# Attention and MLP in one kernel: MLP groups of six chunks, up products that change PSUM banks half way, probability products in batches of two to four key blocks

## The chip, the core and the metric

The kernel runs on one core of one Trainium2 chip, in one launch. The metric is the device time of that launch in microseconds (us), given as the median of several runs. A profiled execution of the same program gives the trace that is read below; its engines are PE (TensorE: matrix products, with its weight loads listed apart as PEld), DVE (VectorE), ACT (ScalarE), POOL (GpSimd) and SP (SyncE, whose queue issues nearly all DMAs).

## The reference

The input x has 2048 tokens of 576 numbers. Two branches are mixed by a gate per token:

```
g = sigmoid((x * gate_w).sum(-1))
a = attention(x @ wqkv, 32 heads of 18) @ wo
b = gelu_tanh(layernorm(x) @ w1 + b1) @ w2 + b2      (w1: 576 x 4608, w2: 4608 x 576)
out = g * a + (1 - g) * b
```

Attention is a full softmax over 2048 keys for each head. All is float32; the kernel makes its large products out of rounded high parts and rests (hi·hi, hi·lo, lo·hi), so each logical product is three on PE.

## The kernel before

**Stages.** A head (some 216 us) computes q, k, v, the layer norm and the gate. Then comes one long loop of 512 steps: 32 units (a pair of heads and one half of the queries) times 16 key blocks of 128. A tail projects the attention output with wo and adds the MLP branch. The loop is written out in Python, so that the order of every instruction on every engine's queue is fixed when the program is built; each engine takes its instructions in that order.

**A step.** `s2` (L275) makes scores for one key block and 512 queries, two heads side by side on the two halves of PE's rows (a *pair* of products), and ACT takes their exponentials (L278) into a tile of a ring of four, `p_of(n) = RING[n % 4]`. It does so twice per step. After each `s2` stands one *round* `s1_round` (L230) of a later unit: again two products side by side, whose row maxima DVE takes (`tensor_reduce`, L232). These four products a round share five PSUM banks in turn (`score_bank`). `pv` (L293) multiplies the probabilities of several finished steps by v. It uses PE as four column strips of 32, where everything else in the loop uses two row halves of 64. It comes once for every `span[0]` steps: a *batch*. Before, the span is 2 unless an up pair asks for 3.

**The MLP as filler.** The MLP is a generator, `mlp()`, from which `fill` and `atom` draw pieces between the score products. A piece runs up to the next mark (`cut[0] = 1` at a slot in `ends`). `GAPS = 7` pieces fit in a batch of two steps: two in its first step, four in the second, one before the product with v. The work comes in two kinds of unit:

- An *up pair* (`h_pair`, L494): two chunks of 128 hidden channels for 512 tokens. Row half h makes chunk h alone, over nine input blocks of 64 and three products each: 27 slots of two products side by side, each into its own bank. For this both row halves hold the whole normed input, high and low parts, in two tiles `Y[0]`, `Y[1]`; part of the low half stands in a tile `low` for the first token block.
- A *down pair* (`out_pair`, L582): 128 tokens and the 4 chunks of one group, 24 slots of two products. Here row half h holds half of each chunk, so both halves add to both output banks. They may not write one bank at the same time, so they start on different banks and change over after 12 slots. The change is guarded: ACT's queue holds a `sem_inc` that waits for the two last products of the first half (L589), and PE waits for that semaphore before the first product of the second (`nc.tensor.wait_ge(swap, ...)`). With `TURNS = (3, 6, 12, 18, 21)` and the piece at gap 3 skipped (`skip.add(3)`), one round L230 and one pair L275 stand between the end of the first half and the wait.

The MLP goes by token blocks of 512 (four), in each over nine groups of `G = 4` chunks: two up pairs and four down pairs per group. That is 72 up pairs and 144 down pairs. GELU between them runs on ACT and POOL in several steps, issued by `defer` and `queue_end`, which model time by counted slots. Down sums are added to an SBUF accumulator by DVE after each down pair (L599). Weights are split in the first token block (raw loads, ACT, POOL, and a store to DRAM scratch), and reloaded as w (L139) in the other three: up pairs from a pool of 3 tiles, down chunks from a pool of 4. `prep_w2(i)` asks for a group's down chunks once the group before has finished its down pairs.

**Pace.** `TOTAL` is the MLP's time by the author's slot figures (231 ns an up slot, 131 ns a down slot); the MLP is to end at step `FIN` = 500. From step 489 (`PSTEP`) on the tail's loads and first steps are drawn in.

Of the kernel before, what the change touches and what calls it, by code (L numbers as in the profile page):

```python
# [16 lines left out]
P = 128  # L17
# [10 lines left out]
G = 4  # L28
NFC = F // P
NG = NFC // G  # L30
# [12 lines left out]
GAPS = 7  # L43
ROOM = 1152
TURNS = (3, 6, 12, 18, 21)
TAIL = (6, 12, 16, 20)
BUSY = 20
TOTAL = NB * NG * (G // 2 * 27 * 231 + 8 * 3 * G * 131)
# [4 lines left out]
ORDER = (0, 1, 3, 2)  # L53
# [16 lines left out]
def gated_mix_kernel(ctx: ExitStack, tc: tile.TileContext, x, wqkv, wo, w1, b1, w2, b2, gate_w, out):  # L70
# [41 lines left out]
    low = att.tile([P, 5, TB], F32R, name="low")  # L112
# [154 lines left out]
    def s2(u, kc, qb):  # L267
# [9 lines left out]
        for h in range(2):  # L277
            nc.scalar.activation(p_of(n)[:, qb, h], ps[h], AF.Exp, scale=SCALE)  # L278
# [63 lines left out]
    def mlp():  # L342
        W1, W2, HT = {}, {}, {}
        RAW = {}
        seq = [(tb, g) for tb in range(NB) for g in range(NG)]
        n = len(seq)
        npair = n * (G // 2)
        Y, ACC = {}, {}

        def chunk(q):  # L350

            i, m = divmod(q, G // 2)
            return i, m, seq[i][1] * G + 2 * m


        R1, R2 = [], []
        for raws in (x_tile(), x_tile()):
            R1.append(raws[:, :9 * P].rearrange("p (c n) -> p c n", c=9))
            R2.append([raws[:, 9 * P + k * D:9 * P + (k + 1) * D] for k in range(2)])
# [9 lines left out]
        def load_w1(q):  # L369

            if (1, q) in LOADED or q >= NQ0:
                return
            LOADED[1, q] = slot[0] + LAND
            fc = chunk(q)[2]
            for h in range(2):
                src = w1[:, (fc + h) * P:(fc + h + 1) * P]
                nc.sync.dma_start(raw1(q)[64 * h:64 * h + 64], src.rearrange("(c p) n -> p c n", p=64))
# [15 lines left out]
        def split(table, key, pool, shape, raw, src, scr, then):  # L393

            def first():
                LOAD[raw[0]](raw[1])
                t = pool.tile(shape, F32R, name="w" + str(len(shape)))
                nc.scalar.activation(t[:, 0], src, AF.Copy)  # L398
                bg.insert(0, (any_time, lambda: second(t), queue, 0))

            def second(t):
                pool_op(src.free_size(), nc.gpsimd.tensor_tensor, t[:, 1], src, t[:, 0].bitcast(F32), op=ALU.subtract)
# [30 lines left out]
        def prep_w2(i):  # L433
            for m in range(G // 2):
                q = i * (G // 2) + m
# [25 lines left out]
        def cuts(n, pieces):  # L461

            return {(k * n + pieces - 1) // pieces for k in range(1, pieces)}

        def h_pair(q, last, inner=False):

            i, m, fc = chunk(q)
            tb = seq[i][0]
            while q == 0 and q not in W1:
                cut[0] = 3  # L470
                yield 0
            wt = ready(W1, q)
            del W1[q]
            ps = [psum(ps_w) for _ in range(2)]
            if q == 0:
                slots = [(w_, 0, c) for c in range(9) for w_ in (0, 1)] + [(0, 1, c) for c in range(9)]
            else:
# [869 lines left out]
```

## Time and profile before

| | |
|---|---|
| median of 3 runs | 2212.33 us (2211.47 to 2215.21) |
| profiled execution, its own time | 2212.78 us |
| its span in the trace | 2211.0 us, 1.8 us less |
| PE busy | 2197.4 us, 99% |
| DVE, ACT, POOL busy | 75%, 64%, 45% |
| mean granted TensorE clock | 1.000 |
| DMA moved | 329.74 MB, mean 149 GB/s |

An engine's busy time is the union of its instructions. PE's instructions overlap each other (one begins while the one before still drains), so what a product costs is read from the distance between starts rather than from its own length.

### The profile page before, as it was taken

The numbers are of one execution on the slowest core, as the hardware profiler recorded it, in microseconds if no ns is written. First come the engines' busy times: TensorE is split into PE (matmuls) and PEld (weight loads), VectorE is DVE, ScalarE is ACT, GpSimd is POOL, SyncE is SP. The second block draws the span as 40 slices with busy tenths as digits, with TensorE's granted clock in tenths as the row PEclk, the third lists the DMA queues.
The fourth block names the chain that finished last, engine by engine and source line by source line (L and its number), as shares of the span: only waits on it lengthen the run. The fifth ranks groups of instructions, "written<-read, shape, count | busy, mean of one in ns | idle before, by whom it ended". The sixth has DMA issues, their size and how long they took to land.

```text
span 2211.0 us, 51479 instructions
## 1 busy us (share of the span) xinstructions
PE 2197.4 (99%) x20496; PEld 1578.5 (71%) x20496; DVE 1647.9 (75%) x2888; ACT 1425.9 (64%) x2623; POOL 1003.7 (45%) x1000
## 2 busy tenths in 40 slices
PE   8999999999999999999999999999999999999999
PEld 7877666676667776677766777767776777776668
DVE  6675777777778778777777777777776777777734
ACT  4333777777776666666666666666665666666672
POOL 4331766666664444444444444444444444444800
PEclk9999999999999999999999999999999999999999
DMA  8867655444464623333354424233464333242265
GB/s 263 276 217 224 199 175 156 154 160 151 152 198 139 197 101 123 121 124 105 115 173 150 138 81 136 101 125 101 125 176 146 109 113 120 98 153 101 77 224 169
DMA packets 171640, 329.74 MB, mean 149 GB/s; under 512 B 65314, under 2 KB 91614, under 8 KB 160672
## 3 DMA queue, kind: packets, MB, share of 16 engines
q1 hardware_dynamic: 168850, 322.67, 45.2%
q8 instruction: 161, 2.64, 0.5%
q10 hardware_dynamic: 2454, 3.75, 0.5%
q14 instruction: 79, 0.65, 0.1%
q0 software_dynamic: 96, 0.03, 0.0%
HBM read 234.00 MB, written 96.69 MB: 150 GB/s over the span
## 4 chain that ended last, share of the span: by engine, by line
PE 95%; DVE 2%; DMA 1%; issue 0%; POOL 0%; ACT 0%; SPq 0%; DVEq 0%; ACTq 0%; POOLq 0%
PE ps L293 21%; PE ps L582 21%; PE ps L494 20%; PE ps L275 13%; PE ps L230 11%; PE ps L894 3%; PE ps L1229 3%; PE ps L915 2%; DVE m L232 1%; PE ps L770 0%; DMA p<-in_A_wqkv_dram 0%; DMA big<-y_scr 0%; PE ps L897 0%; PE ps L896 0%; DVE st L857 0%
## 5 line engine op out<-in xcount | busy, mean ns | idle before, releaser
L232 DVE TENSOR_REDUCE m<-ps 128x1 f32<-128x512 f32 x2048 | 1311.3, 684 | 390.3 <-PE ps L230 380.3
L278 ACT ACTIVATE p<-ps 128x512 f32<-128x512 f32 x1048 | 568.3, 597 | 301.7 <-PE ps L275 299.3
L278 ACT ACTIVATE ring<-ps 128x512 f32<-128x512 f32 x1000 | 543.2, 596 | 294.9 <-PE ps L275 291.8
L494 PE MATMUL ps<-big,w 64*128 64x512 f32 x3708 | 569.4, 393 | 0.2 <-issue 0.2
L183 POOL TENSOR_SCALAR zz<-zz 128x512 f32<-128x512 f32 x288 | 178.1, 618 | 743.3 <-ACT zz L547 686.1
L582 PE MATMUL ps<-w,hh 64*128 64x288 f32 x4352 | 477.4, 294 | 1.5 <-DVE x L599 1.5
L275 PE MATMUL ps<-qa,ka 56*128 56x512 f32 x2048 | 448.6, 420 | 1.1 <-ACT p L278 0.3
L582 PEld LDWEIGHTS ps<-w,hh 64*128 64x128 f32 x4352 | 417.2, 186 | 32.5 <-DVE x L599 6.2
L230 PE MATMUL ps<-ka,qa 54*128 54x512 f32 x2048 | 425.6, 397 | 0.1
L494 PEld LDWEIGHTS ps<-big,w 64*128 64x128 f32 x3708 | 369.8, 187 | 66.1 <-issue 0.5
L183 POOL TENSOR_TENSOR zz<-zz,z 128x512 f32<-128x512 f32 x288 | 371.4, 1290 | 24.0
L275 PEld LDWEIGHTS ps<-qa,ka 56*128 56x128 f32 x2048 | 204.4, 184 | 226.3 <-DVE m L232 174.7
L582 PE MATMUL ps<-w,hl 64*128 64x288 f32 x2176 | 339.3, 292 | 0.8 <-POOL hl L183 0.8
L293 PE MATMUL ps<-p,vt 128*32 128x512 f32 x1968 | 239.1, 598 | 0.0
L230 PEld LDWEIGHTS ps<-ka,qa 54*128 54x128 f32 x2048 | 213.4, 184 | 22.6 <-DVE m L232 2.6
L293 PE MATMUL ps<-ring,vt 128*32 128x512 f32 x1872 | 227.6, 598 | 0.0
L582 PEld LDWEIGHTS ps<-w,hl 64*128 64x128 f32 x2176 | 222.2, 184 | 1.2 <-POOL hl L183 1.1
L183 POOL TENSOR_TENSOR hl<-zz,hh 128x512 fp32r<-128x512 f32 x136 | 176.6, 1299 | 11.4
L183 POOL TENSOR_TENSOR w<-x,w 128x576 fp32r<-128x576 f32 (+1 forms) x54 | 98.8, 1842 | 164.1 <-ACT w L398 158.4
L293 PEld LDWEIGHTS ps<-p,vt 128*32 128x32 f32 x1968 | 52.5, 109 | 111.8 <-issue 102.7
L293 PEld LDWEIGHTS ps<-ring,vt 128*32 128x32 f32 x1872 | 49.8, 109 | 106.4 <-issue 106.4
L599 DVE SCALAR_TENSOR_TENSOR x<-ps,x 128x288 f32<-128x288 f32 x256 | 103.6, 446 | 8.8 <-PE ps L582 8.4
(121 smaller groups left out, 1538.2 us busy)
## 6 DMA issues: line engine op xcount, KB each, us to landing
w<-w_scr SPq DMA_DIRECT2D x54, 1152.0 KB
w<-w_scr SPq DMA_DIRECT2D x108, 576.0 KB
x<-in_B_w_dram SPq DMA_DIRECT2D x72, 288.0 KB
w_scr<-w SPq DMA_DIRECT2D x18, 1152.0 KB
w_scr<-w SPq DMA_DIRECT2D x36, 576.0 KB
qa<-qk_scr SPq DMA_DIRECT2D x192, 72.0 KB
ka<-qk_scr SPq DMA_DIRECT2D x84, 144.0 KB
qk_scr<-hh SPq DMA_DIRECT2D x36, 256.0 KB
```

The lines of the kernel that those rows point to most:

```text
L183: fn(*args, **kw)
L230: nc.tensor.matmul(ps, qa[r0:r0 + 54, t * P:(t + 1) * P], ka[r0:r0 + 54, kb * TB:(kb + 1) * TB], start=True, stop=True)
L232: nc.vector.tensor_reduce(M4[u][:, h, t, kb:kb + 1], ps, axis=AX.X, op=ALU.max)
L275: nc.tensor.matmul(ps[h], ka[r0:r0 + 56, kc * P:(kc + 1) * P], qa[r0:r0 + 56, qb * TB:(qb + 1) * TB], start=True, stop=True)
L278: nc.scalar.activation(p_of(n)[:, qb, h], ps[h], AF.Exp, scale=SCALE)
L293: nc.tensor.matmul(OB[u][r:r + 32, :], v[:, k, 19 * h:19 * h + 32], p_of(c)[:, qb, h, :], start=(k == 0), stop=(k == NT - 1))
L494: nc.tensor.matmul(ps[h], wt[w_][r, c, :], y[r, c, :], start=(k == 0), stop=(k == 26))
L582: mm = nc.tensor.matmul(ps[nn][:, :ND], h_[r, tok], w_[p_][r, cs[nn]], start=(k == 0), stop=(k == 6 * G - 1))
L599: nc.vector.scalar_tensor_tensor(dst, ps[nn][:, :ND], 0.5, b2b[:, cs[nn]] if g == 0 else dst, op0=ALU.mult, op1=ALU.add)
L894: nc.tensor.matmul(ps, w_[:, c, ms], big[:, s_, :], start=(k == 0), stop=False)
L915: nc.tensor.matmul(ps[:, :ND], big[:, s_, tok], w_[:, c, cs], start=(k == 0), stop=False)
L1229: nc.tensor.matmul(ps[:, :ND], OT[b][2][:, s_, tok], w_part(w_, c)[:, cs], start=(k == 0), stop=(k == 13))
```

## The change

1. **Groups.** Six chunks (three up pairs) to a group, in the first token block `(2, 2, 2, 3, 3, 3, 3)` pairs. There are now 25 groups in place of 36, so 100 down pairs in place of 144: 88 of 36 slots and 12 of 24. Up pairs stay 72 of 27 slots. The pool of down chunks grows from 4 to 6.
2. **Input once.** Row half h now holds only its own four of the first eight input blocks, high and low parts together in `Y[0]`, and block 8 in both halves. The tile `low` is gone; eight places of `Y[1]` hold hidden chunks of every other group. Both row halves therefore add to both chunks, and an up pair changes banks after 14 of its 27 slots, by the same `exchange` as a down pair. The weights' raw load takes two long and four short DMAs a pair in place of two.
3. **Batches.** `turn_ends` chooses the span of a batch from 2, 3 and 4 where a unit begins at the start of a batch: the one that leaves the MLP nearest to its pace, with `UNEVEN` = 1500 ns against span 2 for an up pair and span 4 for a down pair. The unit is then cut into exactly the `4 * span - 1` pieces of that batch, with a cut at the bank change. `TURNS`, `TAIL`, `skip` and `ORDER` go.
4. **Exponentials behind the product with v.** With span 4 the ring's next tile is one that the batch still reads; `s2` returns its exponentials, which are then issued behind `pv`.
5. In the tail the first block's divisors stand in four small tiles in place of `low`.

```diff
-G = 4
-NG = NFC // G
+GROUPS = [(2, 2, 2, 3, 3, 3, 3), (3,) * 6, (3,) * 6, (3,) * 6]
+SPANS = (2, 3, 4)
+UNEVEN = 1500.0
-TURNS = (3, 6, 12, 18, 21)
-TAIL = (6, 12, 16, 20)
...
+        def exchange(ends):
+            seen = nc.scalar.sem_inc(swap, 1)
+            swaps[0] += 1
+            for mm in ends:
+                behind_of(seen, mm)
+        def turn_ends(steps, half):
+            pos = begun[0] % NT
+            left = 4 * span[0] - 1 - piece[0]
+            if piece[0] == 0:
+                most = 3 if begun[0] >= TWOS else 4
+                can = [c for c in SPANS if c <= most and (pos + c == NT or pos + c <= NT - 2)]
+                then = spent[0] + steps * (231 if steps == 27 else 131)
+                def off(c):
+                    late = then - base - (TOTAL - base) * (begun[0] + c) / FIN
+                    return abs(late) + UNEVEN * (c == (2 if steps == 27 else 4))
+                span[0] = min(can, key=off)
+                left = 4 * span[0] - 1
+            elif left < 4:
+                left += GAPS
+            a = min(max(1, round(left * half / steps)), left - 1)
+            ends = {-(-k * half // a) for k in range(1, a + 1)}
+            return ends | {half - (-k * (steps - half) // (left - a)) for k in range(1, left - a)}
...
+            ends = turn_ends(27, 14)
+            for turn in range(2):
+                if turn == 1:
+                    nc.tensor.wait_ge(swap, swaps[0])
+                steps = [(w_, s_, c) for c in range(4) for w_, s_ in ((wh, 0), (wl, 0), (wh, 1))]
+                steps += [(wh, 0, 8), (wh, 1, 8)] if turn == 0 else [(wl, 0, 8)]
+                for w_, s_, c in steps:
+                    for h in (0, 1) if turn == 0 else (1, 0):
+                        r = slice(64 * h, 64 * h + 64)
+                        nn = h ^ turn
+                        y = Y[0][r, 4 * s_ + c] if c < 4 else Y[s_][r, 8 - 8 * s_]
+                        mm = nc.tensor.matmul(ps[nn], w_[r, 2 * c + nn if c < 4 else 8], y, start=(k == 0), stop=(k == 26))
+                        if k == 13:
+                            ends_at.append(mm)
+                    k += 1
+                    if k == 14:
+                        exchange(ends_at)
...
+                if (n - i) % 2 == 0 and m < 2:
+                    hh, hl = [Y[1][:, 4 * m + 2 * h + k + 1] for k in range(2)]
...
-            if piece[0]:
-                ends = cuts(24, GAPS - piece[0]) | {12}
-            elif rounds:
-                ends = set(TURNS)
-                skip.add(3)
+            steps = 12 * size
+            ends = turn_ends(steps, steps // 2)
...
-                        wp2 = mstack.enter_context(tc.tile_pool(name="m_w2", bufs=4))
+                        wp2 = mstack.enter_context(tc.tile_pool(name="m_w2", bufs=6))
...
-            s2(u, kc, 0)
+            exps = s2(u, kc, 0)
             gap = 4 * (step - begun[0]) - 2
             full = step - begun[0] >= span[0]
+            behind = full and any(p_of(step) is p_of(c) for c in range(begun[0], step))
+            if not behind:
+                exps()
             half_round(step, gap if step else GAPS - 1, full or step == 0)
             if full:
                 pv(begun[0], span[0])
+                if behind:
+                    exps()
-                begun[0], span[0] = step, 2
+                begun[0], span[0] = step, 3 if kc == NT - 3 else 2
```

More of the change, by code (lines that the diff above doesn't have):

```diff
@@ L1260, in fill @@
             piece[0] = gap
[L1261 to L1263 removed]
+            atom()
         elif gap in (3, GAPS):
```

254 lines of the change are left out of this document (128 added, 126 removed).

## The prediction

> **What bounds the kernel now.** I read the page's busy times first, then who waited for whom, then PE's instructions in order of time.
>
> ```profile
> PE 2197.4 (99%) x20496; PEld 1578.5 (71%) x20496; DVE 1647.9 (75%) x2888; ACT 1425.9 (64%) x2623; POOL 1003.7 (45%) x1000
> ...
> L278 ACT ACTIVATE p<-ps 128x512 f32<-128x512 f32 x1048 | 568.3, 597 | 301.7 <-PE ps L275 299.3
> ...
> L494 PE MATMUL ps<-big,w 64*128 64x512 f32 x3708 | 569.4, 393 | 0.2 <-issue 0.2
> ...
> PE ps L582 <- DVE x L599: 1.5, 4, 0.6
> ...
> PEld ps L275 <- DVE m L232: 174.7, 212, 0.8
> PEld ps L582 <- DVE x L599: 6.2, 20, 0.9
> ```
>
> PE is busy 99% of the span, and the largest wait of its products in the loop is 1.5 us in all (a wait's row gives total, times, longest). Weight loads do wait, 174.7 us for row maxima alone, but while earlier products still run. So the time is the sum of PE's slots, and the change, which leaves the count of slots as it is, can only act on what lies between them: the switches to and from the product with v, and new waits. Both are read from the distance between starts in PE's timeline (start, length, engine, line).
>
> ```profile
> 999.70 0.66 PE L494 MATMUL ps<-big,w 64*128 64x512 f32 x4
> 1000.17 0.43 PE L230 MATMUL ps<-ka,qa 54*128 54x512 f32 x2
> 1000.53 1.06 PE L293 MATMUL ps<-p,vt 128*32 128x512 f32 x8
> 1001.42 1.90 PE L293 MATMUL ps<-ring,vt 128*32 128x512 f32 x16
> 1003.25 0.51 PE L275 MATMUL ps<-qa,ka 56*128 56x512 f32 x2
> 1003.59 0.44 PE L582 MATMUL ps<-w,hh 64*128 64x288 f32 x4
> ...
> 1008.19 0.41 PE L230 MATMUL ps<-ka,qa 54*128 54x512 f32 x2
> 1008.53 1.92 PE L293 MATMUL ps<-p,vt 128*32 128x512 f32 x16
> 1010.39 0.49 PE L275 MATMUL ps<-qa,ka 56*128 56x512 f32 x2
> 1010.72 0.43 PE L582 MATMUL ps<-w,hh 64*128 64x288 f32 x4
> ...
> 1011.12 0.40 PE L230 MATMUL ps<-ka,qa 54*128 54x512 f32 x2
> ```
>
> Two up slots take 1000.17 - 999.70 = 0.47, so 0.235 each, and a pair of score products elsewhere the same. In front of a product with v the pair takes 0.34 (1008.19 to 1008.53), behind it 0.33 (1010.39 to 1010.72): 0.10 more each. The product with v takes 1.86 for two steps (x16 products) and 2.72 for three (x8 + x16): 0.86 a step and 0.14 left over that does not grow. **A batch costs 0.35 us whatever its length** (0.34 by the batch of two, 0.37 by the batch of three, whose pairs take 0.36 and 0.34).
>
> The Trainium skill (TensorEngine Tiling, Key Properties) says that changing the tiling mode drains TensorE; the loop changes from two row tiles to four column tiles and back. By that rule alone only the two 0.10 would be saved and the 0.14 would be the products' own; the trace goes further, since the 0.14 is the same for 16 and 24 products. With 0.20 a batch in place of 0.35 the sum below would be 2228.
>
> **The batches that go.** The groups of products with v, and the first and the last of them in the timeline:
>
> ```profile
> L293 PE MATMUL ps<-p,vt 128*32 128x512 f32 x1968 | 239.1, 598 | 0.0
> L293 PE MATMUL ps<-ring,vt 128*32 128x512 f32 x1872 | 227.6, 598 | 0.0
> ...
> L293 PE MATMUL ps<-p,v 128*32 128x512 f32 x128 | 15.4, 598 | 0.0
> L293 PE MATMUL ps<-ring,v 128*32 128x512 f32 x128 | 15.4, 598 | 0.0
> ...
> 225.89 1.92 PE L293 MATMUL ps<-p,v 128*32 128x512 f32 x16
> ...
> 2160.93 2.29 PE L293 MATMUL ps<-p,vt 128*32 128x512 f32 x16
> ```
>
> Between these two the trace holds 205 batches of 16 products and 34 of 24, 239 in all (205 x 16 + 34 x 24 = 4096, the four groups' sum). After the change every unit that begins at a batch's start fills just that batch: 72 up pairs and 100 down pairs make 172 batches. The MLP is paced to end at step 500, and the last 12 steps take some six batches more: 178. The lengths agree with that: by the planner's figures a step is worth 1804 ns, so an up pair (27 x 231) is due 3.5 steps and takes three or four in turn, about 30 of 72 taking four; a down pair of 36 slots is due 2.6 and takes two or three. 239 - 178 = 61 batches at 0.35 is **-21.4 us** (-20.7 to -22.6 by 0.34 and 0.37).
>
> **The bank change.** Its price shows in the down pairs, of which each has one:
>
> ```profile
> L589 ACTq EVENT_SEMAPHORE  x144: 17/17/17, 255.6 to 2121.7; - x144
> ...
> PEld ps L582: 1.2, 6
> ```
>
> Only 6 of 144 made PE's loads wait. The timeline of a covered one (first lines) and of two exposed ones:
>
> ```profile
> 1058.14 0.30 PE L582 MATMUL ps<-w,hl 64*128 64x288 f32 x2
> ...
> 1058.28 0.41 PE L230 MATMUL ps<-ka,qa 54*128 54x512 f32 x2
> ...
> 1058.52 0.40 PE L275 MATMUL ps<-qa,ka 56*128 56x512 f32 x2
> ...
> 1058.76 0.43 PE L582 MATMUL ps<-w,hh 64*128 64x288 f32 x4
> ...
> 1059.03 0.29 PE L582 MATMUL ps<-w,hl 64*128 64x288 f32 x2
> ...
> 255.27 0.29 PE L582 MATMUL ps<-w,hl 64*128 64x288 f32 x2
> ...
> 255.67 0.30 PEld L582 LDWEIGHTS ps<-w,hh 64*128 64x128 f32 x4 [0.16 <-ACTq L589]
> ...
> 256.04 0.30 PE L582 MATMUL ps<-w,hl 64*128 64x288 f32 x2
> ...
> 1707.19 0.29 PE L582 MATMUL ps<-w,hl 64*128 64x288 f32 x1
> ...
> 1708.09 0.30 PE L582 MATMUL ps<-w,hl 64*128 64x288 f32 x2
> ```
>
> Covered: a round L230 and a pair L275 stand between the halves, and the next half begins at once (two slots, 1058.76 to 1059.03, are 0.27). Exposed: only one pair stands between. From the last slot of the first half to the third of the second should be 0.13 + 0.235 + 0.27 = 0.635; it is 0.77 at 255.27 and 0.90 at 1707.19, where the row halves ran a slot apart. So **0.135 to 0.265 us is lost when one pair covers**, and nothing with two.
>
> In the new code no piece is skipped. The change always falls on the end of a piece, and between two pieces of a batch stands either one round or one pair. For every common shape the first half gets an even number of pieces (4, 6 or 8), so what follows is the next pair L275 alone. All 172 units now have such a change, the 72 up pairs for the first time. An up slot's products are longer than a down slot's (393 ns in its group above against 0.29 us), but its slot is longer by as much (0.235 against 0.133), so the price carries over. I take 0.15, near the low end, because row halves that run apart are the exception: 172 x 0.15 = 25.8, less the six of before (1.2): **+24.6 us**. Ends: -1.2 if it is covered after all, +44.4 at 0.265 each. Behind the waiting semaphore ACT holds the next exponentials, but their products come only with the pair that covers; PE is the one who pays.
>
> **Tighter rounds in long batches.** DVE and ACT rows of the same stretch:
>
> ```profile
> 1002.52 0.68 DVE L232 TENSOR_REDUCE m<-ps 128x1 f32<-128x512 f32 x1
> ...
> 1011.55 1.29 DVE L232 TENSOR_REDUCE m<-ps 128x1 f32<-128x512 f32 x2 [0.98 <-PE ps L230]
> ...
> 1007.29 0.63 ACT L545 ACTIVATE zz<-zz 128x512 f32<-128x512 f32 x1
> ```
>
> A round's first bank is free 0.43 (1011.12 to 1011.55) + 0.68 = 1.11 after its products start, and of five banks the next round's second product needs it. A product that had to wait starts 0.11 behind its load (255.67 above, and the slot after it): 1.22 at best. An up pair in 15 pieces puts three slots between two rounds in three places: 3 x 0.235 + 0.47 = 1.17. That is 0.05 to 0.11 short, in two or three places of some 30 batches: 3 to 10 us; I take **+5** (0 if the lag is lost in the bank change). All other shapes keep 1.25 or more.
>
> **Edges of units.** Down pairs now always begin behind a product with v, which hides the eviction L599 of the pair before; the load rows above show 6.2 us of such waits, 1.5 of them on PE, and there are 44 units fewer: **-2** (-6 to 0).
>
> **Costed at nothing.** The extra copies and DMAs of the first token block are covered by PE's slots of an up pair (27 x 0.235 = 6.3 us); uncovered, as in the fourth rival. The eviction of sums falls from 288 to 200 on DVE (two a down pair), which does not bound. The exponentials behind the product with v wait only for its first products and end inside it.
>
> **Sum.** 2212.78 (profiled execution) - 21.4 + 24.6 + 5 - 2 = 2219.0; the profiled run is 0.45 above the median of 2212.33, so **2218.5**, slower by 0.3%. A measurement of this kernel can tell about 0.2% (4.4 us) from no change.
>
> **The rivals.**
>
> *The bank change costs PE nothing (the other side, 2195).* Weight loads run a slot ahead, and 174.7 us of their waits before cost no product; if in dense batches PE is held at the same place by a bank anyway, the semaphore is set by then. Then only the first term and 2 or 3 us are left: 2212.8 - 21.4 - 1.2 + 5 - 2, some 2193 to 2197. It turns faster than before by 0.2% from under 0.10 us a change. Against: the rows at 255.27 and 1707.19.
>
> *ACT is late at the change (2237).* Slots for GELU steps now lie between the exponentials and the semaphore in ACT's order. Five such steps an up pair are 360, over four issue slots in each of 512 steps about one in six; each takes 0.63 (L545 above): 172 / 6 x 0.63 = 18 on top. The Trainium skill (TensorE: Matmul & The Clock Gate, the table at its head) calls ScalarE's queue strictly first in, first out, which speaks for this rival; the order that no row shows yet is that of a semaphore behind a running GELU step.
>
> *The exponentials wait for the whole product with v (2241).* Then the pair behind lacks a bank for 0.60 (597 ns, L278 above) and the 0.11 of a load, less its own 0.1: 0.65 x 34 batches of four = 22. Against: each writes a quarter of a tile that the batch reads first.
>
> *Weights come late (2238).* Six chunks in place of four, 3.5 MB, are asked for as one batch or two ahead of their use, and in the first block each raw chunk is split on POOL as well. The row of their DMAs, and a stretch of 3 us in which they run:
>
> ```profile
> w<-w_scr SPq DMA_DIRECT2D x108, 576.0 KB
> ...
> 721.00:724.00 3.00, 3.00 (x30) 2.65 (x26) 2.53 (x4) 1.89 (x4) 0.00 (x0) 1.00 1.02 384
> ```
>
> At 384 GB/s (last number) that is 9 us against some 12 for an up batch. Should it miss by 3 us in the seven tightest groups (four in the first block, three ends of blocks), +20.
>
> *The planner does not make long batches (2227).* If it falls behind its pace and stays on short spans, some 205 batches remain: 34 x 0.35 = 12 instead of 21.
>
> **Chances.** Forecast 0.44, in its own range of 2212 to 2225; covered change 0.28; late ACT 0.11; exponentials 0.06, weights 0.06, planner 0.05. Of the forecast 0.24 lies within 0.2% of before (up to 2216.8) and 0.20 above; the covered case is the one that is faster, and the other four add 0.28 to slower. So faster 0.28, same 0.24, slower 0.48. The range for eight in ten must hold the covered case, the forecast, the planner's case and late ACT: 2193 to 2237.
>
> **What would show it.** Batches: 178 groups of products with v, up to 32 products long, each still 0.35 above 0.86 a step. Bank change: some 172 event semaphores on ACT, with PE's loads waiting behind nearly all of them and about 0.15 us lost in each; under 0.1 would make me wrong on the sign. Rounds: loads of L230 waiting for DVE in up batches of four steps. ACT, weights: PE's waits naming GELU steps or DMAs. If the median falls below 2208, the second term was mis-sized.

## The result

| | before | after |
|---|---|---|
| median | 2212.97 us | 2288.15 us (2283.0 to 2290.28) |
| profiled execution, its own time | 2212.78 us | 2283.0 us |
| span in the trace | 2211.0 us | 2281.2 us |
| mean granted TensorE clock | 1.000 | 0.989 |
| batches of products with v in the loop | 239 | 178 |

The changed kernel takes 1.0334 times as long (95% interval 1.032 to 1.0348): 75 us more, where 6 were forecast. The changed kernel's lines are numbered anew: L227 is the round, L272 the pair, L292 the product with v, L525 the up slot, L613 the down slot, L475 the semaphore of the bank change, L276 the exponentials, L406 ACT's copy that begins the split of a raw down chunk, L403 the same for a raw up load, L387 the raw down load, L180 POOL's helper, L626 DVE's eviction of a down pair.

PE is still the bound. The page of the changed kernel, busy times and two groups (busy, mean ns, idle before and what ended most of it):

```profile
PE 2228.4 (98%) x20496; PEld 1596.6 (70%) x20496; DVE 1611.7 (71%) x2800; ACT 1419.1 (62%) x2636; POOL 1005.6 (44%) x1018
...
L525 PE MATMUL ps<-big,w 64*128 64x512 f32 x3888 | 620.7, 397 | 0.6 <-DVE x L626 0.3
...
L613 PE MATMUL ps<-w,hh 64*128 64x288 f32 x2816 | 329.2, 298 | 19.3 <-POOL w L180 14.0
```

The count of products is the same (20496). New is the last row: down products that stood idle for POOL. Where that happens is told by stretches of 200 us. First the kernel before, then after; the columns are each engine's busy time and count, the granted clock, the share of DMA and GB/s.

```profile
200.00:400.00 200.00, 198.05 (x1841) 140.94 (x1841) 146.22 (x251) 142.91 (x254) 126.16 (x108) 1.00 0.55 173
400.00:600.00 200.00, 199.92 (x1959) 138.00 (x1955) 156.37 (x268) 149.71 (x271) 129.86 (x117) 1.00 0.46 152
600.00:800.00 200.00, 199.70 (x1950) 140.02 (x1948) 153.91 (x264) 139.22 (x258) 104.50 (x106) 1.00 0.55 174
```

```profile
200.00:400.00 200.00, 188.37 (x1676) 132.76 (x1676) 137.61 (x232) 134.26 (x251) 123.18 (x115) 0.97 0.55 175
400.00:600.00 200.00, 190.16 (x1816) 133.71 (x1814) 137.80 (x235) 136.55 (x253) 117.67 (x113) 0.97 0.47 147
600.00:800.00 200.00, 185.22 (x1700) 128.74 (x1700) 131.56 (x227) 125.77 (x233) 97.03 (x97) 0.96 0.48 153
800.00:1000.00 200.00, 199.66 (x1971) 139.66 (x1972) 151.29 (x260) 133.82 (x248) 86.57 (x92) 1.00 0.31 100
```

Most of the loss lies in 200 to 800 us; the first token block ends at about 766 us. PE is idle there for 11.6 + 9.8 + 14.8 = 36 us, where before it was idle for 2, and the clock is 0.97, 0.97 and 0.96: (0.03 + 0.03 + 0.04) x 200 = 20 us of PE's work lost to the clock alone. From 800 us on PE is all but full again.

Who was waited for in 240 to 760 us, in the changed kernel (total, times, longest):

```profile
PE ps L613 <- POOL w L180: 17.3, 6, 5.1
PE ps L613 <- ACT w L406: 6.4, 4, 3.0
PE ps L272 <- ACT ring L276: 5.1, 4, 2.8
...
ACT w L406 <- DMA x<-in_B_w_dram: 7.0, 5, 3.9
```

17.3 + 6.4 = 23.7 us of PE's time are waits for the two halves of a split down chunk: the difference on POOL, and the copy on ACT (L406). The 5.1 us are waits for exponentials; with them it is 28.8. How the two hang together is seen in one such wait in order of time:

```profile
376.46 0.39 PE L272 MATMUL ps<-qa,ka 56*128 56x512 f32 x1
...
378.40 0.68 ACT L406 ACTIVATE w<-x 128x576 fp32r<-128x576 f32 x1 [3.85 <-DMA x<-in_B_w_dram]
...
379.62 0.49 PE L272 MATMUL ps<-qa,ka 56*128 56x512 f32 x1 [2.78 <-ACT ring L276]
...
381.20 0.40 PE L613 MATMUL ps<-w,hh 64*128 64x288 f32 x2 [1.09 <-ACT w L406]
...
384.03 0.61 PE L613 MATMUL ps<-w,hh 64*128 64x288 f32 x2 [2.42 <-POOL w L180]
```

ACT waits 3.85 us for a raw chunk's DMA. The exponentials stand behind that copy in its queue, so PE first lacks a bank (2.78), then the chunk's high part (1.09), then its low part (2.42). After it the same products take 0.61 where they took 0.40: the granted clock is 0.54 over 382 to 389 us.

### The profile page after: what moved, and what is told of

Its sections match the earlier page's. It is cut to its first block, busy times and chain, and to the rows that moved or that the text cites. A ratio compares the mean times of both kernels' runs of the same rounds, so it can differ in the third digit from the quotient of the medians.

```text
span 2281.2 us, 51361 instructions
## 1 busy us (share of the span) xinstructions
PE 2228.4 (98%) x20496; PEld 1596.6 (70%) x20496; DVE 1611.7 (71%) x2800; ACT 1419.1 (62%) x2636; POOL 1005.6 (44%) x1018
## 4 chain that ended last, share of the span: by engine, by line
PE 89%; POOL 3%; DVE 3%; DMA 2%; issue 1%; ACT 1%; SPq 0%; POOLq 0%; ACTq 0%; DVEq 0%
PE ps L613 20%; PE ps L292 20%; PE ps L525 19%; PE ps L272 12%; PE ps L227 11%; PE ps L933 3%; PE ps L1270 2%; PE ps L954 2%; POOL w L180 1%; DVE m L229 1%; POOL zz L180 1%; DMA x<-in_B_w_dram 1%; DMA p<-in_A_wqkv_dram 0%; DMA w<-w_scr 0%; DMA bt<-b_scr 0%
## 5 line engine op out<-in xcount | busy, mean ns | idle before, releaser
L276 ACT ACTIVATE p<-ps 128x512 f32<-128x512 f32 x1048 | 568.0, 596 | 333.3 <-PE ps L272 299.1
L276 ACT ACTIVATE ring<-ps 128x512 f32<-128x512 f32 x1000 | 542.5, 596 | 287.2 <-PE ps L272 275.7
L525 PE MATMUL ps<-big,w 64*128 64x512 f32 x3888 | 620.7, 397 | 0.6 <-DVE x L626 0.3
L180 POOL TENSOR_SCALAR zz<-zz 128x512 f32<-128x512 f32 x288 | 178.1, 618 | 776.2 <-ACT zz L585 718.1
L272 PE MATMUL ps<-qa,ka 56*128 56x512 f32 x2048 | 458.9, 420 | 11.1 <-ACT ring L276 5.1
L227 PE MATMUL ps<-ka,qa 54*128 54x512 f32 x2048 | 444.0, 404 | 4.6 <-DVE m L229 4.2
L525 PEld LDWEIGHTS ps<-big,w 64*128 64x128 f32 x3888 | 386.6, 187 | 82.1 <-ACTq L475 19.5
L180 POOL TENSOR_TENSOR zz<-zz,z 128x512 f32<-128x512 f32 x288 | 371.1, 1288 | 24.0
L613 PE MATMUL ps<-w,hh 64*128 64x288 f32 x2816 | 329.2, 298 | 19.3 <-POOL w L180 14.0
L272 PEld LDWEIGHTS ps<-qa,ka 56*128 56x128 f32 x2048 | 211.4, 185 | 189.1 <-DVE m L229 116.5
L613 PEld LDWEIGHTS ps<-w,hh 64*128 64x128 f32 x2816 | 268.7, 188 | 46.2 <-POOL w L180 15.0
L227 PEld LDWEIGHTS ps<-ka,qa 54*128 54x128 f32 x2048 | 225.1, 186 | 38.6 <-DVE m L229 14.1
L292 PE MATMUL ps<-p,vt 128*32 128x512 f32 x1968 | 242.5, 600 | 0.0
L292 PE MATMUL ps<-ring,vt 128*32 128x512 f32 x1872 | 231.6, 597 | 0.0
L613 PE MATMUL ps<-w,big 64*128 64x288 f32 x2304 | 224.9, 300 | 2.8 <-POOL w L180 2.4
L613 PE MATMUL ps<-w,hl 64*128 64x288 f32 x1408 | 225.3, 294 | 0.0
L613 PEld LDWEIGHTS ps<-w,big 64*128 64x128 f32 x2304 | 196.5, 190 | 22.1 <-ACTq L475 7.1
L180 POOL TENSOR_TENSOR w<-x,w 128x1024 fp32r<-128x1024 f32 (+1 forms) x72 | 101.1, 1421 | 185.2 <-ACT w L403 98.0
L613 PEld LDWEIGHTS ps<-w,hl 64*128 64x128 f32 x1408 | 148.7, 187 | 1.7
L292 PEld LDWEIGHTS ps<-p,vt 128*32 128x32 f32 x1968 | 55.0, 109 | 118.5 <-issue 110.1
L292 PEld LDWEIGHTS ps<-ring,vt 128*32 128x32 f32 x1872 | 53.2, 110 | 117.9 <-issue 117.9
```

The lines of the kernel that those rows point to most:

```text
L180: fn(*args, **kw)
L227: nc.tensor.matmul(ps, qa[r0:r0 + 54, t * P:(t + 1) * P], ka[r0:r0 + 54, kb * TB:(kb + 1) * TB], start=True, stop=True)
L272: nc.tensor.matmul(ps[h], ka[r0:r0 + 56, kc * P:(kc + 1) * P], qa[r0:r0 + 56, qb * TB:(qb + 1) * TB], start=True, stop=True)
L292: nc.tensor.matmul(OB[u][r:r + 32, :], v[:, k, 19 * h:19 * h + 32], p_of(c)[:, qb, h, :], start=(k == 0), stop=(k == NT - 1))
L525: mm = nc.tensor.matmul(ps[nn], w_[r, 2 * c + nn if c < 4 else 8], y, start=(k == 0), stop=(k == 26))
L613: mm = nc.tensor.matmul(ps[nn][:, :ND], h_[r, tok], w_[p_][r, cs[nn]], start=(k == 0), stop=(k == steps - 1))
```

## The experiments

"Excess" below is worked out from the trace: for every product of the loop the distance to the next start, less the distance of an undisturbed one of its kind (0.233 us a round or pair, 0.2335 an up slot, 0.1325 a down slot, 0.8585 a step of a batch), added up over stretches of 64 steps. It holds waits, the cost of switching and lost clock alike. The first 128 steps are the first token block. Before has 34 us there, the changed kernel 87, that is 53 of the 70 us by which the spans differ; steps 128 to 512 have 74 and 90.

### First attempts: fewer chunks, an earlier load, a covered change

**e1_first** puts the first block into nine groups of two pairs:

```diff
-GROUPS = [(2, 2, 2, 3, 3, 3, 3), (3,) * 6, ...
+GROUPS = [(2,) * 9, (3,) * 6, ...
...
+  between = {0: pair(q + 1), 1: pair(q + 2, inner=True)} if seq[i][2] > 2 else {1: pair(q + 1, inner=True)}
```

> The first token block goes back to groups of two up pairs (nine of them); all else as changed. Theory W (the down chunks of six-chunk groups are split too late in the first block, PE stalls on them and then runs at half clock): the excess of the first 128 steps, 87 us in the changed kernel against 34 before, falls by some 45; eight units more cost 8 x 0.35 for batches and 8 x 0.2 for bank changes, so about 2245 us, and the granted clock is 1.00 again. Theory B (the bank change and the dense batches are the cause everywhere): the first block keeps its loss, 2280 us or more.

Measured: 2299.14 us, 1.0393 (1.0377 to 1.0408), slower still; the first 128 steps now have an excess of 103. So four chunks instead of six are no cure. In this kernel a group of two pairs has its second up pair between the down pairs of the group before, and only one up pair is left between the request for its down chunks and their first use; in the kernel before there were two.

**e2_raw** counts fewer slots between the raw load and the split, and reloads the raw buffer sooner:

```diff
-LAND = 8
+LAND = 3
...
-defer(3 if looped[0] else ...
+defer((1 if raw[0] == 2 else 3) if looped[0] else ...
```

> Groups as changed; only the raw chunks of the down weights are asked for sooner: one slot after the split that frees their buffer in place of three, and a chunk counts as landed after three slots in place of eight. If what is late is the turn of the two raw buffers (load, wait in counted slots, split), most of the 45 us goes: about 2250 us. If it is POOL's or ACT's work in the first block, the time stays within 10 us of 2288.

Measured: 2301.53 us, 1.0404 (1.0383 to 1.0425). In this kernel's timeline the copy now sits in ACT's queue ahead of the landing:

```profile
377.85 0.68 ACT L406 ACTIVATE w<-x 128x576 fp32r<-128x576 f32 x1 [2.04 <-DMA x<-in_B_w_dram]
388.74 0.68 ACT L406 ACTIVATE w<-x 128x576 fp32r<-128x576 f32 x1 [10.20 <-DMA x<-in_B_w_dram]
...
389.96 1.28 PE L227 MATMUL ps<-ka,qa 54*128 54x512 f32 x2 [9.08 <-ACT ring L276]
```

ACT stands 10.20 us for the DMA, and with it the exponentials; PE waits 9.08 us. That is the strict order of ScalarE's queue of which the Trainium skill (TensorE: Matmul & The Clock Gate, the paragraph on queue depths) speaks: trace and page agree. So the counted delay alone was not the cause: the load itself comes late. SP's queue issues it at 385.06, behind six loads of keys (from 375.25) and the six raw loads of an up pair (377.88 to 384.45).

**e3_cover** puts an empty piece behind the first half of every unit, so that a round and a pair stand before PE waits for the semaphore:

```diff
+            left -= COVER[steps == 27]
             a = min(max(1, round(left * half / steps)), left - 1)
...
                     yield 231
+                    if k == 14 and COVER[1]:
+                        cut[0] = 1
+                        yield 0
```

> Groups as changed; an empty piece behind the first half of each unit, so that a round L227 and a pair L272 both stand between the halves. Theory S (each of the 172 exposed bank changes costs 0.2 us): 36 us of exposed changes go and the tighter pieces give back up to 8: 2252 to 2262 us. Rival (PE would be held there by a PSUM bank anyway): no more than 8 us are won, 2280 us or more.

Measured: 2295.0 us, 1.0375 (1.0359 to 1.039): 7 us more instead of 30 less. Two groups of weight loads in 760 to 2190 us, in the changed kernel and in this one (L525 is L527 there, L272 is L273):

```profile
L525 PEld LDWEIGHTS ps<-big,w 64*128 64x128 f32 x2808 | 277.2, 187 | 58.8 <-ACTq L475 14.1
...
L272 PEld LDWEIGHTS ps<-qa,ka 56*128 56x128 f32 x1490 | 150.4, 184 | 126.6 <-DVE m L229 84.1 <-issue 25.8 <-DVE x L626 1.7
```

```profile
L527 PEld LDWEIGHTS ps<-big,w 64*128 64x128 f32 x2818 | 304.6, 187 | 43.1
...
L273 PEld LDWEIGHTS ps<-qa,ka 56*128 56x128 f32 x1474 | 173.3, 184 | 149.5 <-DVE m L230 108.8 <-issue 25.5 <-DVE dn L316 1.7
```

The wait for the semaphore is gone. The pair, which now follows the round at once, waits for its bank instead: its first bank is that of the round two before, and DVE has not read it. The cover moved the wait.

**e4_both** has both edits of e1 and e3.

> Both: the first block in groups of two up pairs, and an empty piece behind each first half. If the two losses are separate they add: 2245 - 34 + up to 8 = 2211 to 2219 us. If the 61 batches fewer then show, it ends under 2213; if something else was lost too (a late row of maxima at the last block, tighter rounds), it stays above 2220.

Measured: 2302.82 us, 1.0409 (1.0392 to 1.0426). Both theories had fallen alone and fall together.

### Order and shape

**e5_order**: in the first block the second up pair comes behind the four down pairs, after the request for the next down chunks, so that two up pairs lie between request and use.

```diff
-                    between = {1: pair(q + 1)}
+                    between = {1: pair(q + 1)} if seq[i][0] else {}
...
+                if i < n and not last_of(i) and seq[i][0] == 0:
+                    yield from pair(q + 1)
```

> As changed, but in the first token block the second up pair of a group stands behind the group-before's four down pairs again and not between them (as in the kernel before), so that one more up pair lies between the request for a group's down chunks and their first use. Theory O (order): what is late in the first block is this distance: 87 us of excess in the first 128 steps fall to 40 or so, the granted clock returns to 1.00, about 2243 us. Rival (six raw loads a pair and POOL's four splits clog the SP queue whatever the order): within 10 us of 2288.

Measured: 2275.4 us, 1.0285 (1.027 to 1.03): 13 us of the 45 expected. The first 128 steps keep an excess of 77. The waits of down products for split weights do fall, from 23.7 us to 6.3 (200 to 760 us), but others come up: evictions L626 with 4.9, exponentials with 4.4, split up weights with 3.5. Distance alone is no cure.

**e6_order_shape** adds shapes of pieces that leave room for the banks beside an empty piece:

```diff
+SHAPE = {(36, 3): (3, 3, 3, 3, 6, 6, 3, 3, 3, 3), (36, 2): (6,) * 6, (24, 2): (3, 3, 6, 6, 3, 3),
+         (27, 3): (3, 3, 3, 2, 3, 4, 3, 2, 2, 2), (27, 2): (5, 4, 5, 5, 4, 4)}
...
+            if shape:
+                return {sum(shape[:k]) for k in range(1, len(shape))}
...
+                    if k == 14 and covered[0]:
+                        cut[0] = 1
+                        yield 0
```

> The same, with a covered bank change in all units but those in batches of four: an empty piece behind the first half, and the pieces before and behind it made long (nine down slots or five up slots in the two before, six or four in the one behind), so that neither the semaphore nor a PSUM bank is waited for. Theory P (the empty piece alone brought a bank wait of 0.25 us in the place of the semaphore's 0.16 to 0.21, because a round and a pair then follow each other too closely): some 140 changes at 0.18 us go, 2243 - 25 = about 2218 us. Rival (the wait moves on to another place): 2235 us or more.

Measured: 2257.54 us, 1.0202 (1.0187 to 1.0218): 18 us less than e5. Steps 128 to 512 have an excess of 79 (changed kernel 90). With room for the banks the cover does pay.

**e7_order_shape3** forbids spans of four as well.

```diff
+                can = [c for c in can if c < 4] or can
```

> The same, and no batch longer than three steps (every unit covered). The batches of four had uncovered changes (about 30 x 0.2 us) and up pieces with three slots between rounds (bank waits of about 0.1 us): 8 to 12 us less, about 2207 us, with as many batches (178). Rival: the short batches put the MLP behind its pace and the batches grow in number: no gain, 2218 or more.

Measured: 2327.76 us, 1.0526 (1.0508 to 1.0544). With spans of at most three the MLP runs ahead of its pace; its last semaphore comes at 2096.5 us of a span of 2327.2. Then the loop has no filler. The stretch that follows, in this kernel:

```profile
2000.00:2200.00 200.00, 196.57 (x1498) 111.48 (x1498) 143.98 (x247) 118.26 (x222) 39.43 (x43) 0.90 0.14 43
```

1498 products in 200 us, at a clock of 0.90. That says nothing of the price of a batch; without spans of four this planner does not keep the pace.

**e8_batches** puts the new batch rule on the kernel before, with down pairs kept at two steps.

```diff
-            start = begun[0]
-            if start % 2 or (tb > 0 and m == 1 and not inner ...
+            ends = turn_ends(27, 14)
...
-            elif rounds:
-                ends = set(TURNS)
+            ends = turn_ends(24, 12)
```

> The kernel before (groups of four chunks, whole input in both row halves, no bank change in up pairs) with the new rule for batches alone: up pairs fill batches of two to four steps, down pairs always two, shaped as before with an empty piece behind the change. 216 units make 222 batches in place of 239: 17 x 0.35 = 6 us less, about 2206 us. If long batches cost more than their switches (bank waits in up batches of four, exponentials behind the product with v), it is 2212 us or more.

Measured: 2275.18 us, 1.0285 (1.027 to 1.0301), 63 us more than before, with 229 batches where 222 were expected. The excess of the first 128 steps is 67 (34 before), that of the rest some 29 more than before. PE's products wait for exponentials (6.1 us), evictions (5.0), a late row of maxima (4.6), split down weights (4.1) and reloads (2.7). So with groups of four, the order of before and no change of banks in the up pairs, the new batch rule alone makes work on the other engines late. That is a rival for a part of the loss, to which the part on what stays open comes back; of the price of a batch the run says nothing.

### What in the first block: the splits taken away

**e9_down_plain** loads every down chunk as a finished tile (first edit); **e10_all_plain** the up weights too (both).

```diff
-                    split(W2, (q, j), wp2, [P, 2, D], (2, c), raw2(c), w2_scr[c],
-                          lambda c: load_w2(c + 2))
+                    reload(W2, (q, j), wp2, [P, 2, D], plain2(c))
```

```diff
-                split(W1, q, wp1, shape, (1, q), raw1(q), w1_scr[q], lambda q: load_w1(q + 1))
+                reload(W1, q, wp1, shape, plain1(q))
```

> The changed kernel without the splitting of the down weights: every down chunk, in the first token block too, comes by one DMA of the size of a finished tile (from the scratch of normalised tokens, so the output is not the reference's); no raw down load, no copy on ACT, no difference on POOL and no store for them. The up weights are split as before. Theory (the splits of the down chunks, three turns through two raw buffers, are what comes late in the first block, and the half clock follows those stalls): the waits of down slots for POOL and ACT go, about 29 us, and with them most of the 20 us that half clock costs there: 2236 to 2250 us, half clock in the first block under 10 us. Rival (the raw up loads and up splits, or SP's queue, are what is late): no more than 15 us are gained, 2273 us or more, and half clock stays above 25 us.

Measured: 2238.74 us, 1.0114 (1.0098 to 1.0129): 49.4 us less than the changed kernel, by the theory. The three stretches in this kernel:

```profile
200.00:400.00 200.00, 195.28 (x1762) 137.10 (x1764) 146.55 (x250) 134.48 (x251) 108.03 (x104) 0.99 0.51 163
400.00:600.00 200.00, 199.91 (x1962) 140.75 (x1954) 148.20 (x252) 142.05 (x261) 111.55 (x111) 1.00 0.44 140
600.00:800.00 200.00, 198.48 (x1930) 138.96 (x1930) 147.44 (x253) 131.93 (x245) 90.10 (x95) 1.00 0.43 137
```

PE's idle time and the low clock went together: 36.2 us of idle time are 6.3 now, and the 20 us of lost clock some 2, which is 48 of the 49.4.

> As the kernel with plain down weights, and the up weights too come by one finished load a pair in every block, so that nothing is split anywhere (output not the reference's). Theory: the first block now runs like the later ones, excess about 15 us per 64 steps in place of 43: 2228 to 2240 us, and what is left against the kernel before (16 to 28 us) is the price of the new bank changes less the batches saved. Rival (the up splits carry a large part of the loss): at least 20 us below the kernel with plain down weights alone. A second rival (the first block is slow for another cause, such as evictions into the copies of the first block): still over 2260 us.

Measured: 2238.7 us, 1.0115 (1.01 to 1.013), the same as e9. The total hides something here. The scratch from which this kernel takes its weights is written late, so its first up slot starts at 225.5 us and not at 217.2; in the first 128 steps its excess is 34.5 where e9 has 40.8. So up splits may be worth some 6 us, by the trace alone; no total shows it.

### The price of a change of banks

**e11_up_no_change** leaves up pairs in their banks; **e12_plain_no_change** is e10 with the same edit. (The expectation speaks of 86 such changes; there are 72, one for each up pair, and 100 in down pairs.)

```diff
-                    nc.tensor.wait_ge(swap, swaps[0])
+                    pass
-                    for h in (0, 1) if turn == 0 else (1, 0):
+                    for h in (0, 1):
-                        nn = h ^ turn
+                        nn = h
-                    if k == 14:
-                        exchange(ends_at)
```

> The changed kernel with its up pairs left in their banks for all 27 slots: no wait and no semaphore step in the middle of an up pair (each row half then sums only its own part in its own bank, so the output is not the reference's). 86 of the 172 changes go. Theory (a change costs PE 0.2 us each where one pair lies under it): 70 such changes at 0.21 us, 15 us less: 2270 to 2276 us. Rival (what stands there is not the change but the wait of the product of scores for its bank, as covering the change showed): 2282 to 2289 us.

Measured: 2277.86 us, 1.0291 (1.0274 to 1.0309), 10.3 less than the changed kernel. The semaphore's line in the changed kernel, and in this one:

```profile
L475 ACTq EVENT_SEMAPHORE  x172: 17/17/17, 221.9 to 2187.8; - x172
...
  PEld ps L525: 19.5, 71
  PEld ps L613: 16.0, 77
```

```profile
L475 ACTq EVENT_SEMAPHORE  x100: 17/17/17, 258.8 to 2181.7; - x100
...
  PEld ps L611: 16.1, 78
```

> Nothing split and no change of banks in the up pairs, both edits together (output not the reference's). Theory: both gains add, about 50 and 15 us: 2214 to 2226 us, close to the kernel before, the batches saved being about what the other 86 changes cost beside those that the kernel before had. Rival (the change is hidden once the first block runs well): as with plain weights alone, within 4 us of it.

Measured: 2226.54 us, 1.0059 (1.0044 to 1.0074), 12.2 less than e10. 10.3 / 72 = 0.14 and 12.2 / 72 = 0.17 us a change, of 19.5 / 71 = 0.27 us that the loads wait. The stalls of the first block vary by some us between the kernels; the excess of steps 128 to 512, where 52 of the changes stand, falls by 7.7 and 9.9 us, which is 0.15 and 0.19 each.

### Why the splits are late

ACT's copies of raw down chunks in the changed kernel, 425 to 455 us:

```profile
427.45 1.26 ACT L406 ACTIVATE w<-x 128x576 fp32r<-128x576 f32 x2
439.91 0.69 ACT L406 ACTIVATE w<-x 128x576 fp32r<-128x576 f32 x1
441.43 0.70 ACT L406 ACTIVATE w<-x 128x576 fp32r<-128x576 f32 x1
452.48 1.25 ACT L406 ACTIVATE w<-x 128x576 fp32r<-128x576 f32 x2
```

They come in pairs 12 us apart: there are two raw buffers, and each turn runs through copy, difference, load and landing, with the delays that the kernel counts in issue slots (3 before the load, `LAND` = 8 behind it). The kernel before has the same turn (copies at 393.9 and 406.5 us), but two of them a group. Six chunks need three, 25 us from the first copy to the last. **e13_four_raw** is e1 with four raw buffers:

```diff
+            if c >= 4 and c % 4 >= 2:
+                return RT[c // 4][:, c % 2]
...
+                if raw[0] == 2 and done[0] % 4 == 0 and done[0] < NFC:
+                    c = done[0] + 2
+                    RT[c // 4] = wp2.tile([P, 2, D], F32, name="w3")
+                    defer(3, lambda: load_w2(c))
+                    defer(3, lambda: load_w2(c + 1))
```

> The first block in nine groups of two pairs (2299 us when it was run alone), and beside that four raw down buffers in place of two: from the second group on, the third and fourth down chunk of a group are loaded into a tile of the pool of finished down weights, of which nine groups of two leave one free, a whole group ahead. Theory (the turns through two raw buffers are what makes the splits late): the excess of the first 128 steps falls from 103 to under 50 us, 2236 to 2256 us. Rival (one up pair between request and use is too little however many raw buffers there are): 2280 us or more.

Measured: 2243.23 us, 1.0126 (1.0107 to 1.0144): 56 us less than e1, with the excess of the first 128 steps down from 103 to 42. The largest wait of PE's products in 240 to 760 us is now

```profile
PE ps L227 <- DVE m L229: 3.0, 4, 1.7
```

and none that follows it names a weight. So in e1 the turns were the cause: with the same splits, and one up pair between request and use as there, the chunks are in time once they don't go through two raw buffers in turn.

**e14_four_raw_shape** is e13 with the `SHAPE` of e6, **e15_four_raw_order_shape** that with the order of e5.

> Four raw buffers and nine groups of two, and the pieces of the up pairs and down units shaped so that an empty piece stands at the change of banks and the products of scores beside it find their banks free. Theory: the shaping brings 15 to 18 us as it did before, 2222 to 2238 us. Rival (it brought them mostly in the first block, by giving the splits more time): less than 6 us below the version without shaping.

Measured: 2223.28 us, 1.0045 (1.003 to 1.006). Shaping brings 20 us.

> The same with the second up pair of each group of the first block behind the four down pairs, so that two up pairs lie between the request of a down chunk and its use. Theory (turns were the cause, and they are gone): within 6 us of the version without this order. Rival (the distance counts too): 10 us or more below it, 2212 to 2225 us.

Measured: 2222.07 us, 1.0039 (1.0024 to 1.0054), as e14: once there are four raw buffers, distance brings nothing. These two are the best complete versions found, 65 and 66 us below the changed kernel and 10 and 9 above the one before; no version beat that.

### A late row at step 448

In the changed kernel two pairs near 1992 us wait for the row of maxima of their queries; ahead of them, SP's queue:

```profile
1991.74 0.47 PE L272 MATMUL ps<-qa,ka 56*128 56x512 f32 x1 [1.30 <-DMA qa<-mx_scr]
1993.43 0.76 PE L272 MATMUL ps<-qa,ka 56*128 56x512 f32 x1 [1.22 <-DMA qa<-mx_scr]
```

```profile
1979.45 3.12 SPq L136 DMA_DIRECT2D w<-w_scr  x6
1982.62 5.49 SPq L136 DMA_DIRECT2D ka<-qk_scr  x6
1989.28 2.43 SPq L136 DMA_DIRECT2D qa<-mx_scr  x2
```

**e16_row_aside** (on e14) and **e17_plain_row_aside** (on e9) send that row over other queues when down chunks are being reloaded:

```diff
+                        inflow[0] = slot[0]
                         reload(W2, (q, j), wp2, ...
```

> The kernel with four raw buffers, groups of two in the first block and shaped pieces (2223 us), with one line more: where a group's down chunks are reloaded, the mark that sends the rows of maxima over POOL's and ACT's queues instead of SP's for the next 20 counted steps is set. Theory (the row of step 448 is late because it stands behind the reloads and the keys on SP's queue): the stall of 5 us there and the half clock behind it go, 5 to 9 us less: 2214 to 2218 us. Rival (the row waits for its own store, or the transfer itself is slowed by the reloads; or ACT, which then waits for the row, delays the exponentials): 2221 us or more.

> The same line on the kernel with plain down weights (2239 us; output not the reference's). Theory: 5 to 9 us less, 2230 to 2234 us. Rival: 2237 us or more.

Measured: 2223.61 us, 1.0056 (1.004 to 1.0073), and 2238.26 us, 1.0121 (1.0106 to 1.0136): no change in either. In e16's timeline the wait is smaller, one of

```profile
1935.20 0.46 PE L274 MATMUL ps<-qa,ka 56*128 56x512 f32 x1 [0.59 <-DMA qa<-mx_scr]
```

where e14 has two, 2.2 us together, and the half clock behind it is gone. The excess of steps 444 to 452 falls from 5.8 us in e14 to 2.9 in e16, and from 8.2 in e9 to 3.5 in e17. So the place in SP's queue made the row late, but 3 to 5 us there are about as much as these comparisons can tell, and small stalls elsewhere took some of it (2.8 us in steps 504 to 508 of e17).

## Why the prediction was wrong

**Batches: right.** 178 were forecast and 178 are there. A batch of three steps and one of four in the changed kernel:

```profile
1008.17 0.40 PE L227 MATMUL ps<-ka,qa 54*128 54x512 f32 x2
1008.50 1.06 PE L292 MATMUL ps<-p,vt 128*32 128x512 f32 x8
...
1011.21 0.50 PE L272 MATMUL ps<-qa,ka 56*128 56x512 f32 x2
1011.55 0.82 PE L613 MATMUL ps<-w,big 64*128 64x288 f32 x10
```

```profile
838.65 0.49 PE L227 MATMUL ps<-ka,qa 54*128 54x512 f32 x2
839.07 1.92 PE L292 MATMUL ps<-p,vt 128*32 128x512 f32 x16
...
842.64 0.50 PE L272 MATMUL ps<-qa,ka 56*128 56x512 f32 x2
842.98 0.83 PE L613 MATMUL ps<-w,big 64*128 64x288 f32 x10
```

2.71 and 3.57 us are 0.86 a step and 0.13 over, so the fixed part does not grow with length, as argued. Behind the batch a pair takes 0.34, as before. In front it takes 0.33 by the first row, but 0.42 in front of the batch of four, 0.09 more. At 35 batches of four that is some 3 us off the 21. No run isolates the gain as a whole.

**Bank change: right in size for up pairs.** 0.15 us was taken; the runs give 0.14 and 0.17, from whole times. Loads wait at 148 of the 172 changes (71 + 77). For down pairs no run isolates it. That PE gains when the change is taken away rules out the rival of the covered change, and in the changed kernel no wait for the semaphore is longer than 0.3 us, which rules out the rival of ACT being late. (In e2, where ACT stands for a DMA, that rival does come true: products wait 9.8 us for the semaphore, 4.5 in one piece.) What was not seen is that a cover alone brings nothing (e3), because the round and the pair it puts side by side meet in a bank.

**The step that failed: "Costed at nothing", the copies and DMAs of the first token block.** They were said to be covered by PE's slots of an up pair, 6.3 us. The prediction set the work against PE's slots, with no row of a copy, and did not follow the chain through the raw buffers: one turn of two chunks takes 12 us, a group of six needs three, and the change also put the second up pair of a small group between the down pairs of the group before. Taking the down splits away gains 49.4 us, and four raw buffers gain 56 on e1. It had this place among its rivals (*Weights come late*), with the right mechanism in half a sentence, the split of each raw chunk, but priced by the rate of reloads: seven groups by 3 us. Three of the seven were to stand at the ends of blocks, where no product waits for a weight: from 760 us on the down products have no idle time at all. In the first block alone it cost some 29 us of waits (24 for weights, 5 for exponentials) and 20 of clock, two and a half times the rival's price.

**The clock was not in the sum.** In the loop of the changed kernel PE is idle for 42 us, and stretches at half clock that follow cost 24 more, 20 of them in the first block; that is the other part of the mis-sizing.

**The other terms.** Tighter rounds: in 760 to 2190 us the rounds wait 3.4 us for DVE (none before), which fits +5; no run isolates it. Edges: products' waits for the eviction fall from 1.5 us to 0.3, inside the range given. The rivals of the exponentials and the planner play no part: behind 760 us no product waits for an exponential, and batches reach four steps.

**What stays open.** Without down splits the kernel is 26.6 us above before, not 6. By the trace alone some 6 of that are up splits, 3 the late row, 3 the batches of four, and about 7 half clock (13.7 us of it in e9's loop, none before, half lost); these overlap, and no run tells them apart. The excess of steps 128 to 480, counted by kind of product, says where the later blocks lose (65.5 us before, 84.0 in the changed kernel). The batches with the pairs beside them fall from 56.8 us for 159 to 46.7 for 118, so 10 us are saved where 41 x 0.35 = 14 were due. Everything else rises from 8.7 to 37.3: 8.0 of it at the up slots, which is 0.16 for each of the 51 changes of banks there, the rest at score products and down slots, where changes of banks, tighter rounds and the late row mix. The share of the new batch rule, which cost e8 63 us, stays open too. e14 has the same rule and is 10 us above before, so the 63 are not the price of the rule as such, but what it meets in e8 was not looked for by a run.

## What to carry to other kernels

A stage that prepares data once must be costed as a chain through its buffers (load, landing, split, release), by turns, not by the length of its copies: with two buffers, half as many chunks again cost a whole turn more. When a wait is covered by moving other work under it, look at what the moved work waits for in turn. And a kernel that keeps PE 99% busy has a clock to lose: here a stall of 1.5 to 2 us could cost about as much again.

## What the runs showed of the hardware

In e9 a round waits for DVE, with one product standing 1.46 us; the windows around it show the clock:

```profile
1563.32 0.39 PE L227 MATMUL ps<-ka,qa 54*128 54x512 f32 x1
1565.17 0.50 PE L227 MATMUL ps<-ka,qa 54*128 54x512 f32 x1 [1.46 <-DVE m L229]
```

```profile
1563.00:1566.50 3.50, 2.04 (x22) 1.50 (x20) 3.43 (x7) 1.80 (x4) 2.67 (x3) 1.00 0.03 5
1566.50:1569.90 3.40, 3.40 (x28) 3.23 (x26) 1.70 (x3) 2.21 (x5) 3.15 (x5) 0.50 0.05 10
1569.90:1573.00 3.10, 3.10 (x36) 1.74 (x37) 2.83 (x6) 1.37 (x3) 2.87 (x3) 1.00 0.00 0
```

A wait of 1.46 us is followed, 1.3 us after PE is at work again, by 3.4 us at 0.50: 1.7 us more, about the stall's own length. In the changed kernel seven such stretches stand in the loop, of 3.4, 6.8 or 10.2 us, whole multiples, 47.8 us in all. Not every such wait is followed by one: a round of the changed kernel that waits 1.39 us, up to 1611.19, is not (granted clock 1.00 from 1606 to 1620 us). The Trainium skill (TensorE: Matmul & The Clock Gate, Part 1) tells of a half clock after at least one idle window of about 3.4 us; the length of the stretch agrees with that window, but here PE was never idle for a whole one, so the measurement says that a shorter gap can do it, though it need not.
